# Two-step high and low halves for the weights and for q and k of the first batch's later pairs, with a new searched order

## The chip, the cores and the metric

The kernel runs as one program on one core of a Trainium2 chip. The metric is the device time of one execution in microseconds (us); the time before is the median of three runs. Everything said of the inside of an execution comes from one profiled execution of the kernel before.

## What is computed

The reference is a clustered attention followed by a feed-forward layer with a maximum over three products. q, k and v have 4 batches, 8 heads, 768 rows and 64 columns, all float32.

```python
q_assign = argmax(einsum('bhsd,hcd->bhsc', q_n, c_n))   # q_n, k_n, c_n: rows divided by their norms
k_assign = argmax(einsum('bhsd,hcd->bhsc', k_n, c_n))
scores = where(q_assign[..., :, None] == k_assign[..., None, :], scale * q @ k.T, -1e9)
attn = softmax(scores)
x = (attn @ v).transpose(0, 2, 1, 3).reshape(3072, 512)
h = maximum(maximum(x @ w1, x @ w2), x @ w3)            # w1, w2, w3: 512 x 768
return h @ w_out                                        # w_out: 768 x 512
```

## The kernel before

**Precision.** TensorE multiplies float16 here. Each float32 operand is scaled by a power of two and split in a high half, the value rounded to float16, and a low half, the rest. A product is then three matmuls: high by high, high by low, low by high. The split is elementwise work for three engines: VectorE (DVE), ScalarE (ACT) and GpSimd (POOL).

**The work.** A pair is two heads of one batch; there are 16. `prep` (line 718) loads q and k of a pair transposed, finds the power of two (`mx`, `part`, `cut`, a small matmul `mm` that spreads it, `get_p`, `get`), splits, and finds each row's cluster (`mask_rows`, line 559), whose one-hot rows are appended to q and k so that the score matmul adds the mask. `weights` (line 1090) loads 18 pieces of 128 x 512 of w1, w2, w3 and 6 of w_out, and splits them through `split16` (line 1076). `tile_units` (line 1289) does one tile of 128 queries by 768 keys: score matmuls (lines 1307 and 1309), a scaling pass on DVE that also gives the row's extreme (line 1318, called the eviction below: 192 of them, one a tile), the exponential on ACT (line 1324), the split, and a transposition by DMA or TensorE. `visit` (line 1169) multiplies a pair's tiles by v (lines 1242 and 1253), and `ffn` does the hidden layer (line 1479) and the output (line 1537) of 384 rows. The first hidden layer needs pieces of the weights, and all of the first 200 us hold the weights' split besides the attention.

**What sets the order.** Each piece of work is a unit added by `add`; a unit may name several engines that can do it. `Plan.run` emits the units in the order of the table ORDER, and takes the engine of each such unit from the letters of HANDS (V for DVE, S for ACT, G for POOL, Q for the DMA queue of SyncE). Both tables were made by a search. Each engine works through its own instructions in that order, and waits at one whose input is late.

**What the change touches.** In `split16` three units: `sc` scales the piece in place (lines 1079 on ACT, 1081 on the others), a cast to float16 makes the high half (`half`, lines 1025 and 1027), and `low` subtracts (line 1084). In `prep` the units `sc` (lines 832 and 834), `hi` (through `scaled`, lines 378, 380 and 382) and `lo` (line 840) do the same for q and k, but the first pair of the first batch (`fast`) already goes another way: `hi_s` scales and rounds in one instruction, `lo_s` scales and subtracts in one on DVE (line 826).

Of the kernel before, what the change touches and what calls it, by code (L numbers as in the profile page):

```python
# [27 lines left out]
1 2 0 3 4 6-12 16 18 13 17 28 19-21 55 5 14 57 15 22 56 42 29 23-25 27 26 30 58 32 43 59 44 60 61 186 45 33 62  # L28
46 39 187 63 31 64 47 188 159 161 89 192 90 189 170 48 65 66 49 34 38 40 36 41 67 68 77 71 50 160 78 162 35 69
70 91 37 52 51 935 92 72 93 79 80 940 936 73 81 94 124 74 945 95 193 54 937 53 941 942 82 96 938 939 83 163 97  # L30
84 98 943 126 944 194 99 946 75 947 955-957 950-952 960 125 948 164 165 104 86 87 961 76 88 949 127 128 85 190
962 166 958 959 965 980 953 954 191 129 167 105 106 101-103 981 130 131 982 210 966 168 132 975 985 976 986 977
# [6 lines left out]
1038 1039 309 1056 222-224 1057 1065 1014 1048 1066 1067 310 231 1060 1070 1061 1062 1071 1072 1049 311 312 1068  # L39
1058 1075 179 228 1069 1059 225 313 314 229 1080 237 226 176 232 1076 1077 1081 1082 1050 230 227 180 1085 233  # L40
1051 315-317 1052 177 1086 1095 1096 1083 234 235 1053 1084 318 319 236 238 1101 320 1097 1078 1073 1079 321
# [9 lines left out]
1192 409 2590 437 1175 438 1168 1212 2594 406 439 339 340 440 1179 299 350 1202-1204 2595 301 304 407 1176 1213  # L51
# [6 lines left out]
372 481 2620 376 1259-1261 373 1255 363 1229 1265 364 514 2624 1227 1228 449 419 420 418 417 515 1279 482 377  # L58
# [3 lines left out]
1322 1272 493 1314 1273 488 489 1323 422 423 1275 1274 522 1315 1316 1324-1326 1276 1308 424 490 494 1317 518  # L62
# [1543 lines left out]
```

## Time and profile before

| | us |
|---|---|
| median of 3 runs | 698.51 (697.08 to 698.73) |
| the profiled execution | 697.5 |
| its span, first to last instruction | 695.7 |
| TensorE matmuls busy (PE) | 663.6 (95%) |
| VectorE (DVE) busy | 581.9 (84%) |
| ScalarE (ACT) busy | 474.5 (68%) |
| GpSimd (POOL) busy | 405.2 (58%) |

Busy times are of the whole span; the same engine can be full in one stretch and have room in another, so the stretches are to be read apart. A line such as L1084 is a line of the kernel; where a helper does the work, the line is the helper's.

### The profile page before, as it was taken

What the parts mean: (1) busy time and instruction counts of PE and PEld (TensorE: products, weight loads), DVE (VectorE), ACT (ScalarE), POOL (GpSimd) and SP (SyncE); (2) the same over time, 40 slices, a digit from 0 to 9 for tenths busy, and PEclk for the clock granted to TensorE, in tenths of its full rate; (3) what the DMA queues carried; (4) which work ended last, traced back from release to release, by engine and by line L of the source; (5) the groups of instructions that cost most, each with busy time, mean ns of one, the idle gap of its engine ahead of it and who ended that gap; (6) DMA issues with size and microseconds to landing.
All of it is one profiled execution on the core that took longest, in us unless ns stands there. A gap on an engine that the chain in (4) does not pass through costs nothing.

```text
span 695.7 us, 13063 instructions
## 1 busy us (share of the span) xinstructions
PE 663.6 (95%) x4503; PEld 382.4 (55%) x4503; DVE 581.9 (84%) x1345; ACT 474.5 (68%) x886; POOL 405.2 (58%) x432
## 2 busy tenths in 40 slices
PE   4699999999999999999999999999999999999998
PEld 1355556655555546555555555655555555565654
DVE  5999999999898998999998878989998888874231
ACT  7999999999867658877866659676565655652000
POOL 2666887778877436487662548767766744551100
PEclk9799999999999999999999999999999999999999
DMA  6756479898988989999989999999998688767002
GB/s 232 226 174 176 140 178 234 210 183 165 196 174 173 213 187 196 176 215 193 195 164 179 182 174 179 203 207 175 218 176 163 129 166 137 164 118 129 1 1 75
DMA packets 272787, 117.88 MB, mean 169 GB/s; under 512 B 254288, under 2 KB 256464, under 8 KB 272720
## 3 DMA queue, kind: packets, MB, share of 16 engines
q1 hardware_dynamic: 272720, 117.05, 80.5%
q8 instruction: 35, 0.57, 0.3%
q14 instruction: 32, 0.26, 0.1%
HBM read 33.06 MB, written 6.29 MB: 57 GB/s over the span
## 4 chain that ended last, share of the span: by engine, by line
PE 51%; DVE 18%; ACT 10%; DMA 9%; issue 6%; POOL 4%; SPq 1%; DVEq 0%; ACTq 0%; POOLq 0%
PE one L1479 23%; PE one L1537 8%; PE big L1253 7%; PE big L1307 5%; DVE big L1318 5%; PE big L1309 5%; DMA pt<-e 4%; ACT e L1324 3%; POOL e L1330 2%; DMA stage<-in_qk_dram 1%; DMA qk<-cl_t 1%; PE big L1362 1%; PE big L1242 1%; DVE cl_t L571 1%; DVE e L1398 1%
## 5 line engine op out<-in xcount | busy, mean ns | idle before, releaser
L1318 DVE TENSOR_SCALAR_CACHE_REDUCE big<-big,nsc 128x768 f32<-128x768 f32 x192 | 191.6, 1017 | 11.7 <-PE big L1309 9.6
L1479 PE MATMUL one<-x,w16a 128*128 128x384 f16 x1152 | 196.7, 326 | 0.3 <-DVE wf_h L1493 0.3
L1479 PEld LDWEIGHTS <-w16a 128*128 128x128 f16 x1152 | 111.9, 98 | 75.0 <-issue 1.3
L1330 POOL TENSOR_TENSOR e<-e 128x768 f16<-128x768 f32 x73 | 121.0, 1658 | 34.2 <-ACT e L378 29.2
L1324 ACT ACTIVATE e<-big,nm 128x768 f32<-128x768 f32 x116 | 104.3, 900 | 42.0 <-DVE big L1318 24.6
L1307 PE MATMUL big<-qk 128*128 128x512 f16 (+1 forms) x384 | 95.2, 330 | 10.7 <-DVE vmax L954 5.5
L1479 PE MATMUL one<-x,w16b 128*128 128x384 f16 x576 | 99.1, 326 | 0.4 <-DVE vf_h L1493 0.4
L1324 ACT ACTIVATE big<-big,nm 128x768 f32<-128x768 f32 x76 | 66.3, 872 | 43.3 <-DVE big L1318 32.1
L1309 PE MATMUL big<-qk 96*128 96x512 f16 (+1 forms) x384 | 95.0, 328 | 0.2 <-POOL qk L663 0.2
L1253 PE MATMUL big<-pt,v 128*64 128x384 f16 x1008 | 87.9, 327 | 0.5 <-ACT e L1324 0.3
L1398 DVE SCALAR_TENSOR_TENSOR e<-big,rs,e 128x768 f16<-128x768 f32 x72 | 72.4, 1012 | 11.0 <-ACT e L380 10.2
L1479 PEld LDWEIGHTS <-w16b 128*128 128x128 f16 x576 | 55.7, 98 | 38.9 <-issue 2.2
L1253 PEld LDWEIGHTS <-v 128*64 128x64 f16 x1008 | 57.3, 110 | 29.5 <-issue 7.4
L380 ACT ACTIVATE e<-big,rs 128x768 f16<-128x768 f32 x58 | 51.4, 896 | 18.6 <-DMA pt<-e 5.4
L1307 PEld LDWEIGHTS <-qk 128*128 128x128 f16 x384 | 35.2, 98 | 41.6 <-issue 12.4
L1309 PEld LDWEIGHTS <-qk 96*128 96x128 f16 x384 | 37.7, 98 | 26.6 <-issue 1.0
L840 POOL TENSOR_TENSOR qk<-stage,qk 128x768 f16<-128x768 f32 x28 | 46.5, 1663 | 8.5 <-ACT qk L378 5.9
L1537 PE MATMUL one<-wo,vf_h 128*128 128x512 f16 x216 | 48.4, 379 | 0.0
L1537 PE MATMUL one<-wo,wf_h 128*128 128x512 f16 (+1 forms) x234 | 48.3, 362 | 0.0
L1389 POOL TENSOR_SCALAR e<-e,rs 128x768 f32<-128x768 f32 x30 | 27.5, 919 | 30.5 <-DVE rs L1351 14.4
L382 POOL TENSOR_SCALAR e<-e 128x768 f16<-128x768 f32 x37 | 31.0, 839 | 24.2 <-ACT e L1387 7.6
L1493 DVE SCALAR_TENSOR_TENSOR wf_h<-one,wf_h 128x384 f32<-128x384 f32 x48 | 26.3, 549 | 20.9 <-PE one L1479 20.6
(198 smaller groups left out, 1047.9 us busy)
## 6 DMA issues: line engine op xcount, KB each, us to landing
stage<-in_qk_dram SPq DMA_DIRECT2D x32, 384.0 KB, 4.3
wd<-in_w_in_dram SPq DMA_DIRECT2D x18, 512.0 KB, 3.8
stage<-in_v_dram SPq DMA_DIRECT2D x16, 384.0 KB, 4.1
out_dram<-o SPq DMA_DIRECT2D x23, 256.0 KB, 2.9
qk<-qk SPq DMA_DIRECT2D x15, 384.0 KB, 4.6
qk<-qk SPq DMA_DIRECT2D x30, 192.0 KB, 3.6
wd<-in_moe_w_out_dram SPq DMA_DIRECT2D x6, 512.0 KB, 4.5
qk<-cl_t SPq DMA_DIRECT2D x60, 48.0 KB, 2.0
```

Of the source, the lines that this page charges most:

```text
L380: eng.activation(out, x, AF.Copy, scale=k)
L382: eng.tensor_scalar(out, x, k, 1.0, op0=ALU.mult, op1=ALU.mult)
L840: eng.tensor_tensor(t()[:, AQ, i], x(), t()[:, BQ, i], op=ALU.subtract)
L1253: nc.tensor.matmul(t()[D * i : D * i + D, 0:nb], v()[:, i, kt, a], pts[i % len(pts)]()[:, rows[i], c * QT + kt, :], start=(m == 0), stop=( ...
L1307: nc.tensor.matmul(t()[:, lo:hi], aq[:, qs], ak[:, lo:hi], start=True, stop=False)
L1309: nc.tensor.matmul(t()[:, lo:hi], bq[0:K2, qs], bk[0:K2, lo:hi], start=False, stop=True)
L1318: nc.vector.tensor_scalar(s, s, -SCALE if exact else nscs[:, b, pr : pr + 1], 3.0e38, op0=ALU.mult, op1=ALU.min, accum_out=nm())
L1324: nc.scalar.activation(e(), t()[:, 0:S], AF.Exp, bias=nm(), scale=-1.0, accum_out=r)
L1330: eng.tensor_tensor(hv()[:, 1, :], e(), hv()[:, 0, :], op=ALU.subtract)
L1398: eng.scalar_tensor_tensor(hv()[:, 1, :], e(), r(), hv()[:, 0, :], op0=ALU.mult, op1=ALU.subtract)
L1479: nc.tensor.matmul(t()[:, 0:nb], w16[jt // JA][:, jt % JA, wa, i, ct], x16[b, gi, ct]()[:, xa, 0:nb], start=(m == 0), stop=(m == 3 * CT - 1),)
L1537: nc.tensor.matmul(t()[:, lo:hi], h16(jt)[:, ha, tt * P : (tt + 1) * P], wo16[0][:, jt, wa, lo:hi], start=(m == 0), stop=(m == 3 * JT - 1),)
```

## The change

For the weights, the scale is folded into both halves. The high half is made by one instruction that scales and rounds. The low half is one instruction on DVE that scales and subtracts; on POOL it is two, a scaling in place and a subtraction. For q and k of the first batch's pairs 1 to 3 the same is done. Pairs of the later batches, and v, keep the three steps. ORDER and HANDS are replaced as a whole.

```diff
 ORDER = """
-1 2 0 3 4 6-12 16 18 13 17 28 19-21 55 5 14 57 15 22 56 42 29 23-25 27 26 30 58 32 43 59 44 60 61 186 45 33 62
...
 HANDS = """
-SSGSSGSSSSSSVVGSSSSSGSGSSGQQGVSSGGGGGGQQGVVSVSSGSGGQQVGVGSGGSGVSGSSGSGSVSSGSSGGGGSGGVGSGGSGGSGSGSVSSGSGGGSGGSSVG
...
+SSVSSGSSSSSSVVSSSSSSSGGGQQGVSSGGGGQQGVVVSSGSGQQVGVGSGGGGVSGSSVSGSVSGSGSVSSGVSGGGGGSGGVSVSGSGGSSVSVSGSVGSSVSVSVSG
...
+            def hi_2(eng, hi_s=hi_s):
+                hi_s(eng)
+
+            def lo_2(eng, i=i, x=x, lo_s=lo_s):
+                if eng is nc.vector:
+                    lo_s()
+                else:
+                    eng.tensor_scalar(x(), x(), sm("q_s", 1), 1.0, op0=ALU.mult, op1=ALU.mult)
+                    eng.tensor_tensor(t()[:, AQ, i], x(), t()[:, BQ, i], op=ALU.subtract)
+
...
+            elif not b:
+                h = add({"ACT": 0.84, "POOL": 0.95, "DVE": 0.53}, 0, hi_2, [u], [x, small, t], base, port=True)
+                after = [h, u_cl] if raw else [h]
+                l = add({"POOL": 2.5, "DVE": 0.93}, 0, lo_2, after, [x, small, t], base, port=True)
             else:
...
     def split16(x, x_lease, s, s_lease, hi, lo, deps, prio):
-        def sc(eng):
-            if eng is nc.scalar:
-                eng.activation(x(), x(), AF.Copy, scale=s())
+        def f_hi(eng):
+            scaled(eng, hi(), x(), s())
+
+        def f_lo(eng):
+            if eng is nc.vector:
+                eng.scalar_tensor_tensor(lo(), x(), s(), hi(), op0=ALU.mult, op1=ALU.subtract)
             else:
                 eng.tensor_scalar(x(), x(), s(), 1.0, op0=ALU.mult, op1=ALU.mult)
-
-        def low(eng):
-            eng.tensor_tensor(lo(), x(), hi(), op=ALU.subtract)
-
-        u = add({"POOL": 0.67, "ACT": 0.62, "DVE": 0.39}, 0, sc, deps, [x_lease] + ([s_lease] if s_lease else []), prio, port=True)
-        u = add({"ACT": 0.53, "POOL": 0.6, "DVE": 0.33}, 0, half(hi, x), [u], [x_lease], prio, port=True)
-        return add({"POOL": 1.12, "DVE": 0.6}, 0, low, [u], [x_lease], prio, port=True)
+                eng.tensor_tensor(lo(), x(), hi(), op=ALU.subtract)
+
+        held = [x_lease, s_lease] if s_lease else [x_lease]
+        u = add({"ACT": 0.62, "POOL": 0.67, "DVE": 0.39}, 0, f_hi, deps, held, prio, port=True)
+        return add({"POOL": 1.8, "DVE": 0.6}, 0, f_lo, [u], held, prio, port=True)
```

The new tables move instructions in the whole program. Three places matter below. Lines of the changed kernel are 3 lower than before down to `prep`, and 11 to 12 higher from there.

DVE at the start, before: the first pair's power of two (q_m, q_p, q_r, q_s), the cluster centres' low half (cw), and the first transposition of cluster scores (cl_t).

```order
L752 TENSOR_SCALAR q_m<-q_m_163 128x1
L756 TENSOR_SCALAR q_m<-q_m 128x1
L486 SCALAR_TENSOR_TENSOR cw<-one,cw 64x4x16 x4
L571 STREAM_TRANSPOSE cl_t_194<-big 128x512
L766 TENSOR_REDUCE q_p<-one 128x2
L773 RECIPROCAL q_r<-q_p 128x2
L774 TENSOR_TENSOR q_r<-q_r,hsel 128x2
L770 SCALAR_TENSOR_TENSOR nsc<-q_p 128x1
L775 TENSOR_REDUCE q_s<-q_r 128x1
L571 STREAM_TRANSPOSE cl_t_194<-big 128x256
```

The same place in the changed kernel:

```order
L749 TENSOR_SCALAR q_m<-q_m_171 128x1
L753 TENSOR_SCALAR q_m<-q_m 128x1
L568 STREAM_TRANSPOSE cl_t_184<-big 128x256
L763 TENSOR_REDUCE q_p<-one 128x2
L770 RECIPROCAL q_r<-q_p 128x2
L771 TENSOR_TENSOR q_r<-q_r,hsel 128x2
L772 TENSOR_REDUCE q_s<-q_r 128x1
L379 TENSOR_SCALAR qk<-stage_163,q_s 128x768
L767 SCALAR_TENSOR_TENSOR nsc<-q_p 128x1
L823 SCALAR_TENSOR_TENSOR qk<-stage_163,q_s,qk 128x768
L568 STREAM_TRANSPOSE cl_t_184<-big 128x512
```

The four instructions on cw now stand 30 rows later, the smaller transposition (256 columns) comes first, and DVE makes a high half itself.

ACT at the start, before: maxima of q and k (L744), a load of its function table (L453), cw's high half (L482), the first pair's high half (L380), and copies of it to other partitions (L871).

```order
L744 ACTIVATE qk,q_m_163<-stage_160 128x768
L744 ACTIVATE qk,q_m_163<-stage_167 128x768
L453 ACT_TABLE_LOAD
L453 ACTIVATE warm<-c_ss 128x1
L482 ACTIVATE cw<-one 64x4x16 x4
L744 ACTIVATE qk,q_m_184<-stage_176 128x768
L744 ACTIVATE qk,q_m_184<-stage_192 128x768
L380 ACTIVATE qk<-stage_167,q_s 128x768
L871 COPY qk<-qk 64x768
L1062 CAST top<-wd 128x512
L871 COPY qk<-qk 64x768 x5
L832 ACTIVATE stage_192<-stage_192,q_s 128x768
```

And in the changed kernel:

```order
L450 ACT_TABLE_LOAD
L450 ACTIVATE warm<-c_ss 128x1
L741 ACTIVATE qk,q_m_171<-stage_163 128x768
L741 ACTIVATE qk,q_m_171<-stage_165 128x768
L741 ACTIVATE qk,q_m_179<-stage_173 128x768
L377 ACTIVATE qk<-stage_165,q_s 128x768
L741 ACTIVATE qk,q_m_179<-stage_186 128x768
L1073 CAST top<-wd 128x512
L882 COPY qk<-qk 64x768 x3
L479 ACTIVATE cw<-one 64x4x16 x4
L741 ACTIVATE qk,q_m_248<-stage_245 128x768
L882 COPY qk<-qk 64x768
```

The table load stands ahead of the first maxima, cw's high half behind the first copies, and only one maximum of the second pair comes before the first high half.

POOL at the first pieces of the weights, before:

```order
L1081 TENSOR_SCALAR wf<-wf,sc_s 128x512
L1064 CAST top<-wd 128x512
L1027 TENSOR_SCALAR w16a<-wf 128x512
L1084 TENSOR_TENSOR w16a<-wf,w16a 128x512 x3
L1162 TENSOR_TENSOR x_844<-xs,x_844 128x384
```

And in the changed kernel, where L1095 is the scaling and L1096 the subtraction of one low half:

```order
L1095 TENSOR_SCALAR wf<-wf,sc_s 128x512
L1096 TENSOR_TENSOR w16a<-wf,w16a 128x512
L1095 TENSOR_SCALAR wf<-wf,sc_s 128x512
L1096 TENSOR_TENSOR w16a<-wf,w16a 128x512
L1174 TENSOR_TENSOR x_844<-xs,x_844 128x384
```

POOL keeps two instructions for a low half that it makes; it makes 14 of the 24 of the weights, and DVE 10 (17 and 7 before).

## Rows read from the trace of the kernel before

**Rows 1.** The page: busy time of each engine, share of the span, instructions

```profile
PE 663.6 (95%) x4503; PEld 382.4 (55%) x4503; DVE 581.9 (84%) x1345; ACT 474.5 (68%) x886; POOL 405.2 (58%) x432
```

**Rows 2.** Busy times by stretch: its length, then each engine's; instructions in brackets

```profile
0.00:25.00 25.00, 10.07 (x26) 2.90 (x27) 17.09 (x48) 19.77 (x35) 9.94 (x41) 0.92 0.72 253
25.00:163.60 138.60, 130.17 (x937) 79.18 (x936) 134.59 (x300) 130.33 (x243) 102.28 (x100) 0.98 0.71 182
163.60:200.00 36.40, 35.76 (x239) 19.39 (x239) 32.97 (x80) 31.83 (x57) 27.79 (x29) 1.00 1.04 195
200.00:675.00 475.00, 470.14 (x3208) 271.28 (x3205) 394.04 (x916) 290.96 (x550) 264.66 (x264) 1.00 0.85 164
675.00:695.70 20.70, 17.44 (x102) 9.68 (x100) 3.18 (x5) 1.63 (x3) 0.51 (x1) 1.00 0.17 63
```

**Rows 3.** In order of time, 6 to 25 us and at 163.6: start, us, engine, what

```profile
6.11 2.78 PE L795 MATMUL big<-stage,cwf 128*64 128x512 f32 x4 [0.67 <-DVE cwf L496]
...
6.89 0.84 ACT L744 ACTIVATE qk<-stage 128x768 f16<-128x768 f32 x1 [1.97 <-DMA stage<-in_qk_dram]
...
7.85 1.28 ACT L453 ACT_TABLE_LOAD   x1
...
8.11 0.15 DVE L756 TENSOR_SCALAR q_m<-q_m 128x1 int32<-128x1 int32 x1
...
8.82 0.29 PE L762 MATMUL one<-ident,q_m 128*128 128x128 bf16 x1
...
10.01 0.73 DVE L486 SCALAR_TENSOR_TENSOR cw<-one,cw 64x64 f16<-64x64 f32 x4 [1.74 <-ACT cw L482]
...
11.41 0.25 DVE L766 TENSOR_REDUCE q_p<-one 128x2 f32<-128x128 f32 x1
...
12.35 0.94 ACT L380 ACTIVATE qk<-stage,q_s 128x768 f16<-128x768 f32 x1 [0.67 <-DVE q_s L775]
...
22.50 0.82 POOL L663 COPY qk<-cl_t 32x768 f16<-32x768 f16 x1
...
24.99 1.02 DVE L1318 TENSOR_SCALAR_CACHE_REDUCE big<-big,nsc 128x768 f32<-128x768 f32 x1
...
163.61 1.01 DVE L1318 TENSOR_SCALAR_CACHE_REDUCE big<-big,nsc 128x768 f32<-128x768 f32 x1
```

**Rows 4.** Groups on DVE: count, busy us, mean ns of one, idle before them

```profile
L1084 DVE TENSOR_TENSOR w16a<-wf,w16a 128x512 f16<-128x512 f32 x2 | 1.4, 686 | 0.0
L382 DVE TENSOR_SCALAR pt<-big 128x768 f32<-128x768 f32 x2 | 1.9, 957 | 0.0
L382 DVE TENSOR_SCALAR rp<-rs 128x6 f16<-128x6 f32 x4 | 2.0, 507 | 0.0
L382 DVE TENSOR_SCALAR xs<-one,vi 128x384 f32<-128x384 f32 x2 | 1.2, 614 | 0.0
L382 DVE TENSOR_SCALAR vf_h<-one 128x384 f32<-128x384 f32 x10 | 5.5, 546 | 0.0
```

**Rows 5.** Single lines on DVE: shortest, median and longest, in ns

```profile
L1068 DVE SCALAR_TENSOR_TENSOR wf<-wd,top x24: 674/684/1752, 17.4 to 141.2; 128x512 int32<-128x512 int32 x24
L774 DVE TENSOR_TENSOR q_r<-q_r,hsel x16: 120/161/1599, 12.0 to 483.0; 128x2 f32<-128x2 f32 x16
```

**Rows 6.** The groups of those two lines, with their means

```profile
L1068 DVE SCALAR_TENSOR_TENSOR wf<-wd,top 128x512 int32<-128x512 int32 x24 | 18.0, 750 | 1.3 <-ACT top L1062 1.2
L774 DVE TENSOR_TENSOR q_r<-q_r,hsel 128x2 f32<-128x2 f32 x16 | 6.0, 377 | 0.2
```

**Rows 7.** Groups on ACT and POOL: scaling and rounding of weights, and POOL's subtractions

```profile
L1079 ACT ACTIVATE wf<-wf,sc_s 128x512 f32<-128x512 f32 x10 | 7.1, 731 | 0.0
L1025 ACT CAST w16a<-wf 128x512 f16<-128x512 f32 x9 | 5.4, 621 | 0.0
L1062 ACT CAST top<-wd 128x512 f16<-128x512 bf16 x14 | 10.9, 780 | 1.6 <-DMA wd<-in_w_in_dram 0.9 <-DMA wd<-in_moe_w_out_dram 0.7
L1330 POOL TENSOR_TENSOR e<-e 128x768 f16<-128x768 f32 x73 | 121.0, 1658 | 34.2 <-ACT e L378 29.2 <-issue 1.4 <-DVE e L382 1.1
```

More of the change, by code (lines that the diff above doesn't have):

```diff
@@ new lines @@
+73 82 120 121 908 917 909 74 101 99 184 102 100 913 914 925 926 160 84 85 83 918-920 930 927 86 928 921-923 122
+161 931 185 929 123 162 124 163 125 924 950 932 935 126 951 952 127 201 168 945 955 946 936 947 937 956 957 169
+938 165 103 107 108 948 949 189 109 128 933 958 934 959 166 953 110 111 129 112 98 113 954 202 105 104 130
+132-134 965 960 939 941 204 106 114 115 118 940 966 190 961 191 203 117 192 193 116 967 962 970 942 205 119 167
+963 207 971 964 990 135 968 972 975 206 991 969 985 995 976 208 170 992 194 986 977 987 136 978 996 993 140-142
@@ new lines @@
+438 439 2653 2654 1347 1342 505 2619 2620 1333 531 1343 1348 1300 477-480 467 509 2621 1310 1327 1365 532 513
+2622 440-442 1366 1349 1382 514 2623 1383 536-538 1301 1302 1350 1334 1335 2624 1367 1368 443 2625 1351 1352
+2626 515 1357 2629 1399 1358 516 1384 517 1369 1374 444 1359 1360 2630 1400 518 2627 1344 511 1336 510 1375 1361
+1376 2655 519 1317 2628 2631 1318 2632 1401 1353 1402 2633 2637 520 521 1362 533 445 1385 1363 2634 2713 1370
+1371 2635 1391 1392 1403 1319 2604 522 1364 525 1354 1393 1394 1377-1380 2636 1355 2638 1386 512 523 524 2639
@@ new lines @@
+2641 534 1372 502 1395 1404 1356 1396 1419 2640 1411 1405 1406 1397 1387 1436 1420 1412 1373 1381 1421 1437 2645
+1428 1388 1389 1413 2642 1414 1422 2643 2644 1438 1407 1398 1415 1439 1429 1423 1416 2646 2647 1417 1390 2648
+1453 1445 1424-1426 2649 1418 1430-1434 1446 1447 1408 1427 1435 1454 1440 540 584 2598 1455 2650 1473 1441 1409
+1456 1442 2651 2652 1443 1457 2656 1474 1448 1410 1444 539 1458 1475 1459 1476 1460 535 1449-1451 2657 1465 1490
+1482 1483 1491 1477 1484 1492 1466 1467 1485 1468 2659 1461 1478 1452 1499 1479 1480 1469 1500 1493 1470 1494
@@ new lines @@
+1486 1471 1487 1501 1488 2662 629 1502-1504 1495-1497 1507 1462 1508-1512 1505 1519 1481 2663 1463 1464 1513
+1489 2658 1536 1527 1520 1528 1537 2665 542 2660 541 2667 1498 1514 1515 1472 2666 1529 543 544 1530 1531 545
+546 1532 1521 547 1522 2668 1538-1540 548 549 551 552 1544 1545 1533 1541 1542 1523 1534 2669 2670 1546 553 2673
+1524 554 2674 1561 2675 1525 1562 1553 2671 1506 1543 1516 1554 1563 1564 555 1565 556 1555 557 1556 2677
+1566-1568 1547 586 1548 1557 1517 1558 2664 1535 585 558 587 1549-1551 2672 2676 1518 2661 1559 561 1560 1569
@@ new lines @@
+656 605 2718 2720 1679 1680 657 1735 1743 680 658 1744 640 1752 1688 1705 1722 1697 2725 681-683 2727 1753 1712
+1745 1713 1736 684 1728 2726 2728 709 648 1760 1761 1754 649 1714 1762 1729 1755-1757 2729 2730 1758 1763 689
+686 687 1746 2733 2734 659 1747 1737 1769-1771 1748 1777 1730 1759 2735 688 1731 1778 2731 1772 2732 2737 710
+1764 2736 2738 1779 690 2741 1765 1738 1749 691 1780 621 622 1739 1740 1773 711 1741 1750 660 623 624 650 663
+662 661 1774 625 712 2742 1775 1732 692 713 714 696 715 719-721 1781 1797 2743 2739 2740 1766 1767 697 1782 1783
@@ new lines @@
+694 1814 1742 2745 1798 1733 626 1799 1789 1776 693 1768 1815-1817 1800 1734 2744 698 2746 2747 1784 699 722
+1751 1785 1790 1831 2749 700 1832 1806 1791-1793 701 2750 1833 627 1794 2748 628 716 2774 1807 1801 1808 1802
+717 2751 1823 1809 1795 2752 702 2759 2753 1796 695 1834 703 1786 1810 1818 685 704 706-708 705 1835 2754 1824
+1811 1836 1812 1825 1803 1826-1829 1787 2755 1804 2757 1837 2756 2758 1838 1819 1851 1813 1843 1805 1852 1820
+1821 2761 1839 1830 1822 1853 1854 1844 2760 1788 1845 1868-1870 1860 2765 2762 1855 1861 1871 1856 1857 1862
@@ new lines @@
+2766 1885 1863-1865 1886 1858 1887 1866 1872 2763 2764 2767 2769 2768 1877 1888 1873 1840 1846-1848 2770 2771
+1874 2721 723 1849 2772 2775 1841 1875 767 1876 1867 2724 1850 1889 1878 1897 2776 1879 1880 1842 1898 1914
+1881-1883 1905 1915 1899-1901 1906 1890 2777 1891 1892 2778 1884 1859 1916 1902 1917 1903 1907 1908 1893 2779
+718 1922 1909 1910 1923 1924 1911 1931 1918 1932 2782 1904 1894 1933 1925 1934 2780 2893 1919 1920 1935 1912
+1926 1936 2833 1937 1895 1896 1913 2783 1927 1939 1959 1951 1940 2785 1928 1929 724 725 1960 1941 1976 1961 1962
@@ new lines @@
+726 1952 727 1938 1942 1943 2786 1963 1930 768 1921 1953 1954 1944-1946 728 1993 1977 1978 2787 1955 1947 1956
+1964 1965 1994 729 730 1995 1968 1969 731 2788 2789 1985 1966 1957 2793 1958 1970 1986 732 2790 1971 769 1979
+770 737 738 1972 1996 734-736 2894 1987 1988 2791 2792 2794 1973 1974 2797 2013 1997 1980 1998 1999 2014 771
+2795 2796 772 1967 2015 1948 1989 1990 2798 739 740 1991 1949 1950 2000 2016 2017 2799 2800 2018 2019 2005 773
+741 1975 1981 1982 812 2801 2022 774 744 775 2006 776 1983 2007 2802 2008-2010 777 2023 2803 2011 2804 2024 2025
@@ new lines @@
+2030 745 2020 2805 813 1992 2026 2031 2027 2047 2806 2028 2809 2067 779 2807 2032 746 747 2048 2068 2781 2001
+2784 1984 2810 2012 2039 2029 2808 748 2033 749 2811 2034 2040 2812 750 782-784 2049 2813 778 2050-2053 751 2069
+2070 752 780 2041-2043 2054 2059 2002 2021 742 815 2035 2044 2003 814 2814 2045 733 2060 2817 857 2004 816 2834
+2084 754 753 755 756 2818 2036 2037 743 2076 2085 2815 2061 2062 2819 781 2086 817 2077 2816 2071 818 2820 2087
+2078 2079 785 2080 2081 2055 786 2046 789 2088 2072 2038 2082 819 2821 2101 790-792 2063 858 820 2102 2103 793
@@ new lines @@
+2227 2164 2238 2197 899 2239 849 2869 2246 2215 2240 876 877 2871 2870 2867 2208 2228 2241 885-887 850 2242 2243
+2873 2868 2216 2247 2237 889 878 2244 2872 851 2255 891 2198 2248 852 853 2874 2256 2257 2875 2263-2265 2249 902
+903 2199 854 810 811 2876 890 888 2200 2217 904 2877 2878 2250 2165 2258 2259 2166 2879 2260 2283 2284 2275 2881
+2245 2251 2285 2252 2286 2261 2880 855 2882 2895 2300 2218 3013 2301 2302 2292 2883 2253 2885 2276 2266-2270
+2277 2219 2220 2293 2287 2254 2262 2317 2294-2296 2271 2278 2886 2297 2318 2279 2298 2280 2303 2319 2884 2288
@@ new lines @@
+SGSSVGGSGVGSVVGGGSSVVGGGGSVSSGGSSSVSSSGVVVSGGGSSVGVSGSGSVSGGGSVVGSSGSVVSSSGSVVVGGSGVSVVGGGSSVVGGGSVSVGGSGSSVVSGG
+SSVSSGGSSVVSGSGSSVGSSGGSVSSSVVVSVGSSGGSVGGGGGSVSGGGSSSVVSSGSVVSSVGVSVGGSGSVSVGSSGVVVSGGGGSVVGGGSGVVSSSGSSVSSGGGV
+VSVSGSVSVSGVGVSVGSGGGVVSSSGVSSVSVGGSVVVSGGSVVVGGGVSSVSGGGVVVSSSVSSVVSGGSGSVSGGGVSVVSGGVSVGGGGSSSVGSVGSSVGSGGGSVG
+GVGSSSVSSSGVSVGGGGSSVSSGVSGSVSSGGVSVGSGGGSVVGSGVSSVVGGGGSVSSSVVSVVGGGVGVVSGSGSSVSSSGVVVSGGGSGVVSVSVGVVSGGVGSVSGV
+GSVSVSGGGVSVVGVVSVVGVVGVSVVSSGGVSVGVGGVSVSSSGVGSVSGGGGSVGGGGVVVVGVGVSVVGGSVVSGSVVGGSVVSVSVVSGSVVSGSSSSVVSVSVVVGS
@@ L168 @@
+VVGVSVVGGSVVGGSVVVVSSSSVVSVSVVGGVVVSGSVVSGSVVSGSVVGGSSSSVVGGSVVGGSVVSGSVVGGVVVVGSVVSVSSSVVVSGVVVSGSVVSVSVVSVVVVG
+VSVVSVSSSVVVGVSVVGGVVVGGSVVSGVVVSGSVVVGSSSSVVSGSVVVGSVVSGSVVVGVVVSGVVVSGVSSVVVGVSVVGVSVVSGSVVSGVVVVGVVVVGVVVS
 """
```

104 lines of the change are left out of this document (32 added, 72 removed), and 107 rows, old and new, of the table ORDER.

## The prediction

> **What bounds the kernel now.** First the busy times of the page: TensorE is busy for 663.6 of 695.7 us, VectorE (DVE) for 581.9 [rows 1]. So 32.1 us of TensorE's span are idle, and a change to elementwise work can win only from these, or from matmuls that stand far apart. Next the same by stretch [rows 2], where the reader should look for the engine that is full. To 25 us TensorE is idle for 14.9 us; from 25 to 163.6 for 8.4; to 200 for 0.6; to 675 for 4.9 out of 475; then 3.3 in the tail. From 25 to 163.6 us DVE is busy for 134.59 of 138.60 us (97%) and ScalarE (ACT) for 130.33 (94%): there DVE sets the pace, ACT follows closely, and TensorE looks full (130.17) only because its matmuls lie thin (937 in 138.6 us, against 3208 in 475 later). From 200 us on TensorE sets the pace, and DVE has 81 us of room. GpSimd (POOL) is at 74% in the DVE stretch and 56% later. The first eviction starts at 24.99, the 49th at 163.61 [rows 3]: the DVE stretch is what lies between them, so a microsecond less of DVE work ahead of the 49th eviction is a microsecond off the time, as long as ACT lets it. After 200 us such a microsecond only adds to room.
>
> **What the change does, part by part.** By name it takes one step of three from 24 pieces of weights and 6 of q and k. In instructions it takes less. On POOL a low half is still a scaling and a subtraction, and in the new order POOL makes 14 of the 24 low halves and all 6 of q and k. So the weights go from 72 instructions to 24 + 10 + 28 = 62, and q and k from 18 to 18. What q and k win is that the high half no longer waits behind a scaling. Over the whole program the new tables take some 6 us from DVE and 8 from ACT and put 14 on POOL (each kind's difference in count times its mean duration; an estimate). Most of that falls after 200 us, where none of the three is full, and I cost it at nothing; the cover is the 4.9 us of idle TensorE there, and what it could cost or give is in the range.
>
> *DVE between the first and the 49th eviction.* Counted in the two orders up to the 49th eviction. Gone: the 7 subtractions of weights at 0.686 us, 2 copies of 768 to pt at 0.957, 4 to rp at 0.507, 2 to xs at 0.614, 2 to vf_h at 0.546, which ACT now makes: 4.8 + 1.9 + 2.0 + 1.2 + 1.1 = 11.0 [rows 4]. New: 10 low halves that scale and subtract. Their nearest row is another two-input instruction of 128 x 512, median 0.684 [rows 5]: 6.8. Further one high half of q and three subtractions of 384 elements, for each of which I take the 0.546 of a pass of 384 [rows 4]: 2.2. A subtraction of 768 goes and one comes. Sum 9.0 - 11.0 = -2.0 us. About eight instructions of under 0.45 us are left out; with them it would be near -3. Bounds 0 (ACT, which takes over the copies, becomes the limit) and -3.
>
> *The start.* The first pair's power of two is cut by 8.26 us, but its small matmul runs at 8.82, behind the cluster products of 512 columns (6.11 + 2.78), and DVE comes to q_p at 11.41 only [rows 3]: it first sits at cw, idle for 1.74 us until ACT has been through its table load (7.85 + 1.28) and the high half of cw. In the changed order cw stands 30 rows later, the table load ahead of the first maximum (ACT has 1.97 us of idle there, until the second input lands at 6.89), and the products of 256 columns come first. q_p can start near 8.75 and the scale be there near 9.7 in place of 12.3. Of this DVE wins the idle 1.74 less a wait of about 0.35 for the small matmul: -1.4 us. The rest was work that is still to be done. The first eviction itself hardly moves (some 1.1 us of small work is put ahead of it, and counted above): near 24.7. Bounds 0 and -2.6 (the whole advance of the scale). What is late next: the last of the four row copies, which POOL ended at 23.3 and which ACT now makes behind nine other things; by the length of such a copy (0.82) it can cost what the start gives.
>
> *Collisions.* A tiny product on DVE (128 x 2) takes 0.161 us as a rule, and up to 1.599; the two-input instruction at L1068 0.684 and up to 1.752 [rows 5]: about a POOL subtraction (1.658 [rows 7]) held them up. Over all 24 + 16 the means lie 24 x 0.066 + 16 x 0.216 = 5.0 us above the medians [rows 6], 0.13 each. Up to the 49th eviction the change has five more such instructions on DVE (10 + 3 new, 7 weights' and one of rp gone): +0.7. Bounds 0 and 5.3 (1.07 each).
>
> The Trainium skill (SBUF — State Buffer, Who interferes with whom) says that a DVE instruction with two SBUF inputs and a POOL instruction that reads SBUF block each other fully, whichever starts second. By that rule, with POOL reading for 74% of the time and half a subtraction (0.83) to wait, each would cost 0.6 us, the five 3.1, and the sum would come out near the time of before; the rows give a quarter of that price, since most two-input instructions stand at their median. The rule is the mechanism of the slower rival.
>
> *ACT.* Up to the 25th exponential it makes four scaled high halves of weights (0.731) in place of two scalings and five casts (0.621), -1.6 us, but three more casts of raw weights (0.780, +2.3) [rows 7], and copies taken from DVE. The net is about +1.4, and it is 94% busy. Bounds 0 and +1.4; I take +0.4, since by the 49th eviction ACT has less to do than before.
>
> Sum: -2.0 - 1.4 + 0.7 + 0.4 = -2.3 us. The profiled execution took 697.5 us, so it would take 695.2. It lies 1.0 below the median of the three runs, 698.51, and 0.4 above the lowest; for a median I add half of that distance: **695.7 us**. What a measurement of this kernel can tell from no change is about 0.3%, 2.1 us: faster means below 696.4, slower above 700.6.
>
> **The rivals.**
>
> 1. *Nothing gained.* DVE's relief stops at ACT, which is 94% busy in the same stretch and gets work earlier, and the start's advance is lost to the row copies on ACT. For it: 94% next to 97% leaves little. Against it: ACT still has 8.3 us of idle there. Then the terms are 0 to -0.5 and the time 697.5 to 698.5.
>
> 2. *Also the later part gets shorter.* DVE and ACT have less to do after 200 us, and POOL has room (264.66 of 475). If half of TensorE's 4.9 idle us goes, the time is 695.2 - 2.4 = 692.8, as a median 693.3. For it: TensorE's waits there can end only on these or on transfers. Against it: POOL's subtraction takes 1.658 us, longer than DVE's pass of that size, and more of them stand on POOL now.
>
> 3. *Slower: the ten new low halves collide on DVE.* The subtractions they replace run at a mean of 0.686 [rows 4], as short as the median of the other line, so the old order kept them clear of POOL. If the new ten, between 60 and 160 us where POOL is busiest, each wait 0.6 us in the mean, DVE pays 6.0 in place of 0.7: 695.2 + 5.3 = 700.5 for the profiled execution, 701.0 as a median. It decides once some five of the ten are held up by a whole POOL subtraction (1.07 us each: 5.4 against the 3.0 to be won and 2.1 to be seen). For it: POOL has more two-step low halves in the same stretch. Against it: the means of the lines that can collide.
>
> That the change does not do what it says is in the count above: for q and k no instruction goes at all.
>
> **How the numbers follow.** The forecast has 0.46, rival 1 0.26, rival 2 0.15, rival 3 0.13. The forecast reaches 696.4 with its own unknowns (0.7 us away), so of its 0.46 I put 0.37 to faster and 0.09 to no change; with rival 2 faster has 0.52, with rival 1 no change 0.35, slower 0.13. The forecast's own range is 693.7 to 697.5. The range for 8 in 10 goes from just under rival 2, 692.5, to just under rival 3, 700.5.
>
> **What would show it.** The start is right if the first pair's scale is ready by 10 us, DVE's idle time before cw is gone, and the first eviction starts between 24 and 25. The DVE term is right if the 49th eviction starts near 160.5 to 162 with DVE still at 96% or more of the stretch. The collision term is right if the ten new instructions have a mean under 0.82 us; a mean of 1.2 or more is rival 3. If the 49th eviction is as early as said but the end is not, the gain was given back after 200 us, and TensorE's idle time there, 4.9 us now, has grown. If ACT shows 97% of the DVE stretch and DVE falls under 95%, it is rival 1. I am wrong altogether if the first eviction comes later than 26 us, or if the part after 200 us changes by more than 3 us either way.

## The result, and the profile after

The changed kernel took 688.28 us (median of five runs, 685.59 to 689.2) against 698.51 for the kernel before (697.08 to 699.12): a ratio of 0.9845, 95% interval 0.9818 to 0.9872. It is faster by 10 us where 2.8 were forecast, and lies below the range (692.5 to 700.5). The profiled execution took 688.28 us, 9.2 less than that of before. First its page line, as in [rows 1], then the stretches of [rows 2], cut at the same places of the work (the first and the 49th eviction, and so on); columns as there; the last three are the granted share of TensorE's clock, the busy share of the DMA engines, and GB/s.

```profile
PE 659.3 (96%) x4503; PEld 381.7 (56%) x4503; DVE 575.2 (84%) x1324; ACT 464.8 (68%) x884; POOL 423.1 (62%) x442
```

```profile
0.00:23.47 23.47, 9.19 (x27) 2.93 (x28) 18.32 (x54) 20.07 (x35) 12.39 (x41) 0.89 0.76 271
23.47:159.10 135.63, 128.95 (x942) 78.47 (x941) 132.83 (x288) 126.98 (x241) 100.70 (x97) 0.99 0.74 188
159.10:194.00 34.90, 34.68 (x234) 19.07 (x234) 33.54 (x87) 29.46 (x55) 26.63 (x25) 1.00 0.95 186
194.00:665.80 471.80, 469.12 (x3207) 271.56 (x3204) 386.35 (x896) 287.83 (x553) 282.46 (x279) 1.00 0.86 166
665.80:686.50 20.70, 17.38 (x102) 9.68 (x99) 4.16 (x7) 0.47 (x1) 0.91 (x1) 1.00 0.17 64
```

Stretch by stretch against [rows 2]: -1.5 to the first eviction, -3.0 in the DVE stretch, -1.5 to the next cut, -3.2 in the long part that TensorE bounds, nothing in the tail; together -9.2. So the part behind the 49th eviction, which the prediction costed at nothing, gave 4.7, as much as everything before it. There TensorE is busy for nearly as long (523.3 in three stretches before, 521.2 now) and idle for less (8.8 and 6.2). Of the -1.5 behind the 49th eviction 1.1 is busy time: five matmuls of that stretch (239 and 234) are now done ahead of it (937 and 942).

The head and the 49th eviction, in order of time, as in [rows 3]: the scale is ready near 8.1, where DVE starts the first high half, in place of 12.3; DVE goes from q_m to q_p, q_r and q_s with no wait for cw.

```profile
5.38 0.84 ACT L741 ACTIVATE qk<-stage 128x768 f16<-128x768 f32 x1
...
7.16 0.27 DVE L763 TENSOR_REDUCE q_p<-one 128x2 f32<-128x128 f32 x1
...
7.93 0.16 DVE L772 TENSOR_REDUCE q_s<-q_r 128x1 f32<-128x2 f32 x1
...
8.12 0.62 DVE L379 TENSOR_SCALAR qk<-stage,q_s 128x768 f16<-128x768 f32 x1
...
23.46 1.02 DVE L1330 TENSOR_SCALAR_CACHE_REDUCE big<-big,nsc 128x768 f32<-128x768 f32 x1
...
159.12 1.01 DVE L1330 TENSOR_SCALAR_CACHE_REDUCE big<-big,nsc 128x768 f32<-128x768 f32 x1
```

The groups on DVE that answer to [rows 6], and the ten new low halves (L1093); after the bar busy us and the mean in ns:

```profile
L1079 DVE SCALAR_TENSOR_TENSOR wf<-wd,top 128x512 int32<-128x512 int32 x24 | 18.1, 756 | 0.2
...
L1093 DVE SCALAR_TENSOR_TENSOR w16a<-wf,sc_s,w16a 128x512 f16<-128x512 f32 x4 | 3.2, 829 | 0.0
L1093 DVE SCALAR_TENSOR_TENSOR w16b<-wf,sc_s,w16b 128x512 f16<-128x512 f32 x4 | 2.9, 748 | 0.0
L771 DVE TENSOR_TENSOR q_r<-q_r,hsel 128x2 f32<-128x2 f32 x16 | 2.4, 150 | 0.1
...
L1093 DVE SCALAR_TENSOR_TENSOR wo<-wf,r_o,wo 128x512 f16<-128x512 f32 x2 | 2.0, 1011 | 0.0
```

The 24 conversions (L1079, before L1068) stand as before, the tiny products went from 377 ns to 150, and the ten low halves have a mean of 0.83 us: (4 x 829 + 4 x 748 + 2 x 1011) / 10. Two of them were held up by a subtraction of POOL; this is the longer one, with the subtraction in which it began:

```profile
157.61 0.91 POOL L1174 TENSOR_TENSOR vf_h<-vf_h 128x384 f16<-128x384 f32 x1
157.79 1.27 DVE L1093 SCALAR_TENSOR_TENSOR wo<-wf,r_o,wo 128x512 f16<-128x512 f32 x1
```

### The profile page after: what moved, and what is told of

Read it like the earlier page. It is cut to its first block, busy times and chain, and to the rows that moved or that the text cites. A ratio compares the mean times of both kernels' runs of the same rounds, so it can differ in the third digit from the quotient of the medians.

```text
span 686.5 us, 13032 instructions
## 1 busy us (share of the span) xinstructions
PE 659.3 (96%) x4503; PEld 381.7 (56%) x4503; DVE 575.2 (84%) x1324; ACT 464.8 (68%) x884; POOL 423.1 (62%) x442
## 5 line engine op out<-in xcount | busy, mean ns | idle before, releaser
L1342 POOL TENSOR_TENSOR e<-e 128x768 f16<-128x768 f32 x77 | 127.8, 1660 | 35.2 <-ACT e L375 21.0
L1336 ACT ACTIVATE big<-big,nm 128x768 f32<-128x768 f32 x76 | 66.3, 872 | 37.8 <-DVE big L1330 25.6
L1410 DVE SCALAR_TENSOR_TENSOR e<-big,rs,e 128x768 f16<-128x768 f32 x72 | 72.8, 1011 | 7.6 <-ACT e L377 6.6
L377 ACT ACTIVATE e<-big,rs 128x768 f16<-128x768 f32 x52 | 46.5, 897 | 16.1 <-DVE rs L1363 12.1
L1401 POOL TENSOR_SCALAR e<-e,rs 128x768 f32<-128x768 f32 x35 | 32.6, 933 | 29.5 <-DVE rs L1363 11.9
L1505 DVE SCALAR_TENSOR_TENSOR wf_h<-one,wf_h 128x384 f32<-128x384 f32 x48 | 26.5, 552 | 23.1 <-PE one L1491 20.8
L847 POOL TENSOR_TENSOR qk<-stage,qk 128x768 f16<-128x768 f32 x24 | 40.1, 1673 | 6.5 <-ACT qk L375 5.4
L379 POOL TENSOR_SCALAR e<-e 128x768 f16<-128x768 f32 x39 | 32.8, 841 | 14.9 <-DMA pt<-e 7.8
```

The lines of the kernel that those rows point to most:

```text
L377: eng.activation(out, x, AF.Copy, scale=k)
L379: eng.tensor_scalar(out, x, k, 1.0, op0=ALU.mult, op1=ALU.mult)
L847: eng.tensor_tensor(t()[:, AQ, i], x(), t()[:, BQ, i], op=ALU.subtract)
L1336: nc.scalar.activation(e(), t()[:, 0:S], AF.Exp, bias=nm(), scale=-1.0, accum_out=r)
L1342: eng.tensor_tensor(hv()[:, 1, :], e(), hv()[:, 0, :], op=ALU.subtract)
L1410: eng.scalar_tensor_tensor(hv()[:, 1, :], e(), r(), hv()[:, 0, :], op0=ALU.mult, op1=ALU.subtract)
```

## The experiments

"Order" and "hands" are the tables ORDER and HANDS; the cut between early and later part is the unit of the 49th eviction. Each ratio is to the kernel before on the same chip. The last three columns are places in the profiled execution: first eviction, 49th eviction, and the time from there to the end of the span.

| run | median us | ratio (95%) | 1st | 49th | later part |
|---|---|---|---|---|---|
| before | 698.51 | 1 | 25.0 | 163.6 | 532.1 |
| changed | 688.28 | 0.9845 (0.9818 to 0.9872) | 23.5 | 159.1 | 527.4 |
| e1 | 704.87 | 1.0108 (1.0079 to 1.0138) | 24.2 | 169.3 | 532.9 |
| e2 | 703.79 | 1.0089 (1.0063 to 1.0116) | 24.9 | 175.4 | 525.7 |
| e3 | 696.06 | 0.9982 (0.996 to 1.0004) | 23.5 | 165.0 | 531.9 |
| e4 | 699.73 | 1.0035 (1.0017 to 1.0053) | 24.0 | 170.6 | 527.1 |
| e5 | 689.2 | 0.9887 (0.986 to 0.9915) | 23.6 | 159.5 | 526.5 |
| e6 | 697.68 | 0.9997 (0.9977 to 1.0017) | 23.9 | 161.7 | 533.9 |
| e7 | 689.27 | 0.9887 (0.9861 to 0.9914) | 23.6 | 159.3 | 527.5 |
| e8 | 705.43 | 1.0111 (1.0087 to 1.0135) | 23.6 | 169.4 | 534.5 |
| e9 | 778.76 | 1.1167 (1.1121 to 1.1213) | 23.1 | 159.1 | 614.0 |
| e10 | 764.1 | 1.0947 (1.0902 to 1.0991) | 23.1 | 160.1 | 597.2 |
| e11 | 717.4 | 1.0279 (1.0248 to 1.031) | 24.5 | 180.1 | 536.0 |
| e12 | 707.07 | 1.0148 (1.0109 to 1.0187) | 23.5 | 173.8 | 530.7 |
| e13 | 692.71 | 0.9935 (0.991 to 0.996) | 23.8 | 164.6 | 526.3 |
| e14 | 704.63 | 1.0109 (1.0084 to 1.0134) | 23.5 | 167.8 | 534.2 |
| e15 | 698.4 | 1.0009 (0.9995 to 1.0023) | 25.0 | 164.4 | 533.4 |

### Edit and tables apart: e1 to e4

e1, the changed code with the old tables:

```diff
-ORDER, HANDS = new
+ORDER, HANDS = old, without the 30 scaling units
```

> The old order with the new arithmetic alone: the scaling units are taken out, every other unit keeps its place and its engine (a low half on POOL is a scaling and a subtraction there). Theory A (the new order makes the gain, the arithmetic only gave it room): 696 to 699 us, the first eviction near 25.0 us as before, the 49th within 1.5 us of 163.6. Theory B (the shorter split itself makes it): 693 us or less, the 49th eviction before 161 us. My prediction's terms would give no more than 2 us here, since DVE's relief came from its hands in the new order.

e2, the code before with the new tables:

```diff
-ORDER, HANDS = old
+ORDER, HANDS = new, with each scaling unit put ahead of its high half
```

> The new order and engines with the old arithmetic: a scaling unit stands right ahead of each high half, on POOL where POOL makes the low half, else on the engine of the high half. Theory A: 688 to 692 us, the first eviction near 23.5 us. Theory B: 695 us or more. What lies between is the share of the arithmetic inside this order: ACT makes 10 more scalings of 0.73 us (7.3 us) ahead of about 160 us, where it has some 8.6 us of room.

e3, and e4 with "new" and "old" exchanged:

```diff
-ORDER, HANDS = new
+ORDER, HANDS = new up to the 49th eviction, then the units left, as in old
```

> New arithmetic; the new order up to the 49th eviction, the rest in the old order and on the old engines. Theory A1 (the gain is made at the start and in the DVE stretch, and only carried on later): the 49th eviction near 159 us and 692.5 to 694.5 us, since 4.5 us of the 9.2 are there by then. Theory A2 (half or more comes after 200 us, from the relief of DVE and ACT there): the same early part, and 693 or more with TensorE idle 4 to 5 us between 195 and 670 us.

> New arithmetic; the old order up to the 49th eviction, the rest in the new order. The 49th eviction as in the first run of this group. If the parts add up, this run's gain and the third run's gain over the first together make the whole (10 us by the medians): 692 to 695 us. If the late part only catches up what the early part wins (or needs it), 696 or more.

Theories A and B both fall: the edit alone costs 7.5 us, the tables alone 6.4 (e2's time is in B's numbers, but e1 refutes B). e3 has neither theory's early part (165.0), and the parts do not add up in e4 (699.73, its second case). But the last column sorts cleanly in these runs, whatever stands in the early part: 531.9 to 532.9 with the old later order, 525.7 to 527.4 with the new. e2 has three steps and the new later order: 525.7. (Among the later runs e12, with the new later order, lies between at 530.7.) And where e1 loses is plain on DVE. Its stretch between the first and the 49th eviction, and its groups of conversions and of the last low halves:

```profile
24.18:169.29 145.11, 129.16 (x937) 78.26 (x935) 141.59 (x300) 121.68 (x226) 111.89 (x109) 0.99 0.66 175
```

```profile
L1083 DVE SCALAR_TENSOR_TENSOR wf<-wd,top 128x512 int32<-128x512 int32 x24 | 23.1, 962 | 1.4 <-POOL w16a L1100 1.3
L1097 DVE SCALAR_TENSOR_TENSOR wo<-wf,r_o,wo 128x512 f16<-128x512 f32 x3 | 2.9, 986 | 0.0
```

DVE is busy for 141.59 us with as many instructions as in [rows 2], 7.0 more, and ACT is not short (121.68 of 145.11). The 24 conversions alone cost 23.1 - 18.0 = 5.1 more than in [rows 6]. One of them in order of time:

```profile
94.89 1.65 POOL L1346 TENSOR_TENSOR e<-e 128x768 f16<-128x768 f32 x1
...
95.11 1.99 DVE L1083 SCALAR_TENSOR_TENSOR wf<-wd,top 128x512 int32<-128x512 int32 x1
```

POOL's subtraction began 0.22 us earlier; the conversion lasts until 97.10, that is 0.55 us after the subtraction ended. Seven of the 24 are held up by a subtraction like this here, to 1.0 us or more; in the trace of before it is one (the 1752 of [rows 5]).

### Is it chance? e5 to e8

e5 is the changed kernel without an edit; e6 and e7 add the same lines to the kernel before and to the changed one (in the changed one unit 946 is the 8th eviction):

```diff
+            if n == 946:
+                for _ in range(4):
+                    nc.gpsimd.tensor_copy(self.nudge, self.nudge_in)
...
+    plan.nudge, plan.nudge_in = warm, ident[:, 0:1]
```

> The changed kernel once more, without an edit, beside the kernel before on the same chip: how far one execution of it differs from the next. If the moment at which TensorE's clock rises for good (25.1 us in the first profile of the change, 31.3 in that of before) is a matter of the execution, it will differ here, and the 49th eviction will come between 158 and 163 us; the median should be 686 to 690, the ratio near 0.985. If it belongs to the order, it is 25 us again.

> The kernel before with four copies of one column on POOL put behind the 8th eviction, into a tile that nobody reads, less than 1 us of POOL in all, which has 36 us of idle time in the DVE stretch. Theory W (the time is the sum of the work on the full engine): no change, within 0.5 us of before. Theory C (what counts is which two-input instructions of DVE meet a two-input instruction of POOL; the searched order keeps them apart, and any shift of POOL against DVE deals the meetings anew): slower by 2 to 8 us, with the mean of the 24 conversions (684 ns alone, mean 750 before) at 820 or more, and the loss made before the 49th eviction.

> The same four small copies on POOL behind the 8th eviction of the changed kernel. Theory W: within 0.5 us of the changed kernel, 687.8 to 688.8. Theory C: slower than the changed kernel by 2 to 8 us, 690 to 696, with more stretched two-input instructions on DVE before the 49th eviction.

e8 has the new tables up to the first eviction only:

```diff
-ORDER, HANDS = new
+ORDER, HANDS = new up to the first eviction, then the units left, as in old
```

> The two-step split with the new order and hands up to the first eviction, and the old from there. My step on the start by itself: the first eviction comes 1.0 to 1.5 us earlier than before. Theory W: this advance is kept and the rest loses nothing: 696 to 697. Theory C: what follows is the old order at another alignment, so it loses as the old order with the two-step split did (704.9), less the advance: 701 to 704, with the loss before the 49th eviction.

The gain repeats in e5: 8.4 us against the kernel before on that chip (697.56), and 8.3 in e7. Theory C falls in e6 and e7: 0.74 us more on POOL (four copies of 185 ns) changes nothing, and in e7 the five stretched two-input instructions of the changed kernel stand where they stood, within 0.4 us. So the meetings belong to an order of work and not to a tenth of a microsecond. As a second look at the old order, e6 has its 49th eviction at 161.7; with 163.6 and e13's 164.6 the old early part is at 163.3 in the mean, the new at 159.3 (159.1, 159.5, 159.3). e8 goes the way that Theory C said of it, but past its numbers (705.43 against 701 to 704) and for another reason: the early start is gone by the ninth eviction (37.8, as in e1), and the rest loses as e1 does.

The one execution with the whole new early part that stood at 165.0 was e3's, and its runs spread from 693.13 to 699.87. Other work behind that part does not explain it: e9 and e10 below have other work there too, and stand at 159.1 and 160.1. What differs first is TensorE's clock. In each execution the first score matmuls run at half clock (granted 0.50, 1.2 GHz); when the clock comes back to full (1.00, 2.4 GHz) differs. Before from 25.0 us, and changed from 25.1 (the granted clock is third from the end):

```profile
25.00:31.30 6.30, 5.38 (x21) 3.44 (x20) 6.19 (x18) 6.09 (x11) 2.60 (x3) 0.50 0.65 167
```

```profile
25.10:31.30 6.20, 4.93 (x32) 3.11 (x31) 6.18 (x16) 5.93 (x11) 3.39 (x4) 1.00 0.42 134
```

The length of two score matmuls, the next ones behind the first twelve, shows it in every trace. Here are before, e6 and e13 (old early part), then changed, e5 and e3 (new):

```profile
30.68 0.81 PE L1307 MATMUL big<-qk 128*128 128x512 f16 x2
...
28.94 0.49 PE L1311 MATMUL big<-qk 128*128 128x512 f16 x2
...
29.52 0.84 PE L1309 MATMUL big<-qk 128*128 128x512 f16 x2
...
27.95 0.48 PE L1319 MATMUL big<-qk 128*128 128x512 f16 x2
...
28.06 0.48 PE L1319 MATMUL big<-qk 128*128 128x512 f16 x2
...
28.51 0.85 PE L1323 MATMUL big<-qk 128*128 128x512 f16 x2
```

From the first to the ninth eviction the same instructions took 13.2 us in the changed kernel, e5, e7 and e10, where the matmuls are short again by 24 to 27 us, 13.9 in e9 (by 29) and 15.5 in e3 (by 31). The orders alone do not decide it: the old early part has both kinds, and so has the new. So 2.3 of e3's 5.9 us arise there, beside the longer half clock. The rest comes later, where further conversions are held up (their sum is 20.0 in place of 18.1). No run sets the clock, so its share is read from these executions and not tested.

### Order or engines, and the parts of the edit: e9 to e15

e9 and e10:

```diff
-HANDS = new
+HANDS = new up to the 49th eviction, old behind it     (e9, ORDER new)
-ORDER = new
+ORDER = new up to the 49th eviction, old behind it     (e10, HANDS new)
```

> The changed kernel with its own order throughout, but for units emitted after the 49th eviction the engines are those of the old table (352 units change engine). The later part, from the 49th eviction to the end of the span, took 527.4 with order and engines new and 532 to 534 with both old. If the engines make the later gain (TensorE's waits end on DVE, ACT and POOL), it is 531 to 534 here and the time near 694 to 696; if the sequence makes it, 526 to 529 and the time near 689 to 691. The part before is as in the changed kernel, 49th eviction near 159.3.

> The other half: engines of the new table throughout, the new order up to the 49th eviction and the old order behind it. If the engines make the later gain, the later part takes 526 to 529 and the whole 689 to 691; if the sequence makes it, 531 to 534 and 694 to 697. If both runs lose, engines and sequence belong together.

Neither theory's numbers came; the last sentence of e10's did. The later part grows to 614.0 and 597.2. TensorE's waits between 163 and 700 us in e9 (us, times, longest):

```profile
PE big L1321 <- DVE e L1412: 18.7, 19, 2.0
PE big L1321 <- ACT e L1338: 12.2, 10, 2.9
PE big L1321 <- DVE x L1215: 12.0, 6, 5.9
```

So TensorE is bound there only as long as elementwise work is in step; the cover of 4.9 idle us [rows 2] says nothing of how near the waits are.

e11:

```diff
-                eng.tensor_scalar(x(), x(), s(), 1.0, op0=ALU.mult, op1=ALU.mult)
+                nc.scalar.activation(x(), x(), AF.Copy, scale=s())
```

> The two-step split in the old order (704.9), with one edit: where POOL makes a weight's low half, ACT scales the piece in place and POOL only subtracts, as POOL did before. Theory P (in the old order POOL's 17 added scalings of about 0.7 us make it late, and its late subtractions meet DVE's conversions): the conversions' mean goes from 962 ns back to 800 or less, the 49th eviction from 169.3 to 161 to 165, the time to 697 to 700. Rival (the old order is wrong for the new dependences, whoever scales): still 702 to 707.

Theory P's numbers fail, and the run does not decide: it put a new wait in place of the scaling. POOL's waits, 24 to 177 us:

```profile
POOL w16a L1100 <- ACT wf L1099: 15.8, 5, 5.5
POOL w16b L1100 <- ACT wf L1099: 12.6, 3, 6.9
POOL wo L1100 <- ACT wf L1099: 8.1, 2, 6.9
```

e12:

```diff
-HANDS = new
+HANDS = new, with G (POOL) for all 24 low halves of the weights
```

> The changed kernel with all 24 low halves of the weights on POOL: ten two-input instructions of 0.83 us go from DVE, 8.3 us of the full engine, and POOL gets ten more scalings and subtractions, some 18 us, which would fill it to 88% of the DVE stretch. If work on the full engine decides, as my step on DVE reckoned, the 49th eviction comes 4 to 8 us earlier and the time is 680 to 685. Theory P: POOL gets late, the tiles wait for its subtractions and DVE's remaining two-input instructions meet it more often: slower by 3 to 10 us, 692 to 699, with the conversions' mean over 850 ns.

DVE loses 8.3 us of work and the 49th eviction comes 14.7 us later (2.3 of them by the ninth eviction, with TensorE at half clock until 31 us as in e3). Theory P has the direction, but 707.07 is past its 692 to 699. The stretch between the first and the 49th eviction, and DVE's longest waits from 24 to 177 us:

```profile
23.45:173.84 150.39, 133.00 (x935) 81.60 (x934) 132.29 (x278) 127.64 (x241) 115.56 (x113) 0.98 0.63 168
```

```profile
DVE wf L1081 <- POOL w16a L1098: 9.0, 3, 6.2
DVE big L1332 <- PE big L1323: 4.4, 6, 1.2
```

A conversion needs a free piece buffer (there are two, of three pieces each), and POOL gives it free by its low half. DVE was busy for 88% then (132.29 of 150.39), and the conversions still rose to a mean of 957 ns. So a full DVE is a symptom as much as a bound: it is full while POOL keeps up.

e13, the code before:

```diff
-ORDER, HANDS = old
+ORDER, HANDS = old up to the 49th eviction, then the units left, as in new
```

> The kernel before, three steps and all, with its own order and engines up to the 49th eviction, and behind it the later order and engines of the change. No two-step split is left in it. Theory L (the later order, which holds no instruction of the edit, makes most of the gain): early part as before, 49th eviction at 161 to 164; later part 525 to 529; time 688 to 692. Rival (the later gain needs the early part of the change, which hands it work already done, such as six matmuls): later part 530 to 534, time 694 to 698.

The later part is as Theory L said, 526.3; the time is 692.71, 0.7 over its range, since the early part of the profiled execution stood at 164.6. With no two-step split at all, this order gives 4.4 us (697.06 before on that chip). Its later part, and that of before:

```profile
164.64:690.90 526.26, 521.47 (x3542) 300.94 (x3540) 422.76 (x983) 318.05 (x609) 310.45 (x306) 1.00 0.84 164
```

```profile
163.61:695.70 532.09, 523.34 (x3543) 300.35 (x3540) 430.18 (x1000) 324.42 (x609) 292.95 (x293) 1.00 0.84 162
```

TensorE's idle time goes from 8.75 to 4.79 us and its busy time, with one matmul fewer, from 523.34 to 521.47. DVE has 7.4 us less to do there and ACT 6.4 less, POOL 17.5 more; that this is what shortens the waits is not shown. The named waits are small ones of many kinds; before, the first two were these:

```profile
PE big L1307 <- DVE e L1398: 1.8, 2, 1.4
PE big L857 <- ACT e L1324: 1.2, 1, 1.2
```

In the changed kernel both kinds are under 0.3 us, and the largest is a transposition by DMA:

```profile
PE big L1265 <- DMA pt<-e: 1.7, 2, 1.4
```

e14 and e15, the old tables without the scaling units of the part that is split in two steps:

```diff
+split16 as in the change, prep as before     (e14)
+prep as in the change, split16 as before     (e15)
```

> Old order, two steps for the weights alone, three for q and k. The old order with both two-step splits took 704.9. Theory P (POOL's added scalings for the weights shift its subtractions into DVE's conversions): the loss is here, 702 to 706, conversions' mean 900 ns or more. Rival (the split of q and k makes it): 697 to 699.

> Old order, two steps for q and k of the first batch's later pairs alone, three for the weights. Theory P: no loss, 695 to 698, the high halves of the first pairs being ready sooner. Rival: 702 to 706, 49th eviction near 169.

The weights' split makes the loss in the old order (1.0109, as with both), the split of q and k is neutral (1.0009; its 698.4 is 0.4 over Theory P's range). In e14 the conversions and the last low halves read:

```profile
L1070 DVE SCALAR_TENSOR_TENSOR wf<-wd,top 128x512 int32<-128x512 int32 x24 | 21.1, 880 | 1.4 <-POOL w16a L1087 1.3
L1084 DVE SCALAR_TENSOR_TENSOR wo<-wf,r_o,wo 128x512 f16<-128x512 f32 x3 | 2.9, 997 | 0.0
```

The mean is 880 where 900 was expected, 3.1 us more than in [rows 6]; the 49th eviction is 4.2 us later than before.

## Why the prediction was wrong

**The part behind the 49th eviction: costed at nothing, was -4.7 (-3.2 of it after 200 us).** This is the step that failed ("after 200 us such a microsecond only adds to room"). Idle time of TensorE in the long stretch went from 4.86 to 2.68 us; that half was rival 2, to which I gave 0.15, with -2.4. The rest, 1.5 us between 163.6 and 200 and 1.0 of closer matmuls, no case had. The prediction's own sign of being wrong altogether came true: the part after 200 us changed by 3.2. The reasoning took the edit's instructions as the change and the tables as its wrapping. But behind the 49th eviction there is no instruction of the edit: e2 and e13 get the same later part with three steps, and e13 with the old early part too, so it is the tables' doing and not the five matmuls done earlier. What in the new tables shortens TensorE's waits is not settled beyond e9 and e10: order and engines only work together.

**The start: -1.4, and -1.5 in the two profiled executions, but not for its reason.** The scale was ready at 8.1, as said by 10, and the idle time before cw was gone (1.74 to 1.75 us in each of the eight executions with the old order of the start listed below, none in the eight with the new); the first eviction came at 23.46, earlier than the 24 to 25 stated. But the second input's maximum began at 5.38 in place of 6.89 with nothing in the order to cause it. Over eight executions each, the old order of the start had its first eviction at 23.5 to 25.0 (before, e1, e4, e6, e11, e13 to e15; mean 24.2), the new at 23.1 to 23.6 (changed, e3, e5, e7 to e10, e12; mean 23.4). (e2, with the new order but three steps, is in neither count; its one execution stands at 24.9.) So the order's share is near 0.8, the rest a late execution of before, and e8 shows that an early start alone is not kept. I read one execution's landing time as a property of the order.

**DVE in the stretch: -2.0 of work, +0.7 of collisions and +0.4 on ACT, -0.9 in all, was -3.0.** The stretch ended with DVE at 98% and the 49th eviction at 159.1, before the 160.5 to 162 stated. DVE's busy time in it fell by 1.8, but some of that work only moved ahead of the first eviction: over both stretches its busy time fell by 0.5 us (151.7 to 151.2) and its idle time by 4.0 (11.9 to 7.9). So most of the gain up to there is waits that went, not work. The ten new low halves cost more than I took: 740 to 750 ns clear of POOL, and two were held up (1090 and 1274), so 8.3 us in place of 6.8, and their mean of 0.83 us misses the 0.82 named as a sign. The collisions of the older lines did not grow, though: the conversions' sum is 18.1 against 18.0, and the tiny products of the whole program lost 3.6 us. ACT did less up to the 49th eviction, 147.1 us against 150.1, where +0.4 was taken. And TensorE's matmuls do not "lie thin" in this stretch: 937 in 138.6 us and 3208 in 475 are both 6.8 a microsecond, so TensorE was close to being full there too.

Over three executions each the early part moved from 163.3 to 159.3, so -4.0 where start and stretch together were to give -2.3. That is not like with like: all three new executions had the full clock by 28 us, of the old ones only e6. e6 alone, at 161.7, gives -2.4; with the half clock to 30 us and more it is 163.6 and 164.6 (before, e13) against 165.0 (e3), no gain. So the size forecast may be right at an equal clock, but one old execution is too few to show it, and how much of the -4.0 is the order's stays open.

**Rival 3 was the right mechanism at the wrong place.** That the new instructions collide was refuted for this order (0.83 us, against the 1.2 that would have been the rival). For the same edit under the old order it is what happens: in e1 conversions cost 5.1 us more of the 7.0 that DVE is busier, and the run is 7.5 us slower. The prediction priced a meeting as a mean per instruction. The Trainium skill (SBUF — State Buffer, Who interferes with whom) says that a DVE instruction with two SBUF inputs contends with a POOL instruction that reads SBUF, over a pair of ports that is an exclusive lock. The traces agree: the conversions and low halves that a subtraction of POOL held up ended 0.55 us after it, and those that began in its last 0.13 us kept their usual length (but one, which the scaling behind it held up). How many are held up is what the order decides: seven of 24 conversions in e1, one in before.

**Rival 1 is refuted:** ACT is at 94% of the stretch as before, and DVE did not fall under 95%. And the count of instructions, on which I spent the most words, was right and of little weight: the edit without its order costs 7.5 us (e1), and the new order without the edit 6.4 (e2: 49th eviction at 175.4).

## What to carry to other kernels

When a change replaces a searched order as a whole, the order is the change: look at every stretch that it touches, those without an edited instruction first, and give idle time of the bounding engine there a term of its own in the sum. Where two engines hand buffers to each other, work taken from the full one gains only if the other stays in step, as e12 shows with 8 us less on DVE and the 49th eviction 15 us later. And before a row's start time becomes a term, see whether it is the order's or that one execution's, and compare executions whose clock came back at the same place.

## What was not expected of the hardware

A two-input instruction of DVE that begins inside a subtraction of POOL, more than 0.13 us before its end, ends a fixed time after it: 13 conversions and low halves in before, the changed kernel and e1 end 0.546 to 0.553 us after POOL's subtraction, though they are 0.99 to 2.17 us long. A scaling on POOL can do the same: in the changed kernel a conversion that began in one at 70.49 us took 1.14 us and ended 0.54 after it.

The granted clock of a stretch is to be read beside the matmuls. It is 0.89 for the first 23.5 us in the changed kernel's first profile and 1.00 in e5, but two score matmuls take 0.84 to 0.85 us there in both (from 21.2 and 21.3 us on), and 0.48 at 28 us. So e5's 1.00 does not show a full clock there; the length of the matmuls does better.
